# Tiles of one batch each in a sliding-window attention and feed-forward kernel

## The chip, the core and the metric

The kernel runs on one core of a Trainium2 chip. The core has TensorE (matrix products into PSUM), VectorE, ScalarE, GpSimd (POOL in the profile) and SyncE (SP), which has no arithmetic and issues DMAs; ScalarE and GpSimd issue DMAs too. Each engine works through its own instructions in order; semaphores order the engines among each other. The metric is the time on the device in microseconds (us), as a median of several runs.

## The reference

Eight batches of eight heads, 576 rows, head size 64. Each row attends to itself and the 63 rows ahead of it in its own batch; the result goes through a feed-forward block with a gate.

```python
scores = scale * np.matmul(q, k.transpose(0, 1, 3, 2))
rel = pos[:, None] - pos[None, :]
mask = (rel >= 0) & (rel < 64)
attn = softmax(where(mask, scores, -1e9))
x = matmul(attn, v).transpose(0, 2, 1, 3).reshape(4608, 512)
g = x @ w_gate                                  # 512 x 1536
out = (g / (1 + exp(-g)) * (x @ w_val)) @ w_out # 1536 x 512
```

Inputs and output are float32. The kernel computes in bfloat16 and adds up in float32.

## The kernel before, in words

The 4608 rows (8 x 576) are cut into nine tiles of 512 rows in the order of memory. As 576 is no multiple of 512, tile t holds the last 64t rows of batch t-1 and the first 512-64t rows of batch t (`segments`). So a tile's first query block needs the last 64 keys of the tile before it (`kT[(t - 1) % 2]`, line 205 ff.), and one place of the mask moves from tile to tile: GpSimd clears it and restores it in `maskp` (`clear_part`, `restore_part`).

Every tile does the same: load q, k and v; turn q and k so that the head dimension lies on partitions; per pair of heads u (0 to 3) the scores (18 matmuls of 64 keys against 64 or 128 queries, `scores`), exp on ScalarE, the mask; the sums over keys by a product with ones, and their inverse by Ln and Exp on ScalarE (`sums`); the values (16 matmuls, `values`) and the multiplication into `xT`; twelve blocks m of gate and value (`gate_value`, eight matmuls each, then Silu on ScalarE and a multiplication on VectorE into `hT`); four output blocks (`project`, twelve matmuls each). V is held twice: `v1` as it is, and `v2` shifted by 64 rows, so that a window of 128 keys is always 128 partitions; `shift_v` makes `v2` from `v1`.

The order is written by hand; each engine works in the order of the code. The first two tiles (`TURNED = 2`) are loaded as rows and turned on TensorE (`transposes`), and their mask is added in PSUM from `bias`; the later ones are loaded so that VectorE's 32x32 transposition turns them (`load_q`, `load_k`, `turn`), and their mask is a product.

The opening is lines 325 to 437. SP, and ScalarE for some of k, load q and k of tile 0 as float32; ScalarE, VectorE and GpSimd cast them. GpSimd loads tile 1's q and k with a cast on the way (`load_later`), casts v of tile 0, and then loads the weights of gate and value in four blocks of 384 columns with tile 1's v between the second and the third. The shifts of v are DMAs on SP (`shift_dma`). On TensorE eight turns (two tiles, four head pairs) alternate with scores and sums; then come tile 0's values and gate/value blocks 0 and 1. Only after tile 1's last sums does ScalarE load the table for Silu (`set_silu`) and free the PSUM buffers of the gate:

```python
    begun.append(gate_value(0, 1))
    load_qk(2)
    for c in range(2):
        weights_o(6 * c, 6 * c + 6)
    set_silu()
    for m in range(12):
        (begun[m] if m < 2 else gate_value(0, m))()
        if 7 <= m < 11:
            values(1, m - 7, ps_a.tile([P, 2, 512], FP32, name="ao_ps", tag="a")[:, 0])
```

From then on a tile's scores and values alternate with the output blocks of the tile before, and the loads for later tiles stand ahead of the gate/value blocks in GpSimd's and SP's queues. The PSUM buffers: two pairs in `ps_a` (tag a: scores, sums), two each of the tags g and v in `ps_f` (turns, gate, value, output).

Of the kernel before, what the change touches and what calls it, by code (L numbers as in the profile page):

```python
# [8 lines left out]
P = 128  # L9
# [8 lines left out]
def kernel(  # L18
# [14 lines left out]
    TURNED = 2  # L33

# [3 lines left out]
    cast = ctx.enter_context(tc.tile_pool(name="cast", bufs=4))  # L38
# [10 lines left out]
    kT = [cst.tile([P, 4, 512], BF16, name=f"kT{i}") for i in range(2)]  # L49
# [3 lines left out]
    ones = cst.tile([P, D], BF16, name="ones")  # L53
    tri = cst.tile([P, 2, 64], BF16, name="tri")
    bias = [cst.tile([P, 2, 4, 4, 2, 16], BF16, name=f"bias{i}") for i in range(2)]
    maskp = cst.tile([P, 2, 16, 4, 2, 4], BF16, name="maskp")

    def segments(t):

        n0 = 64 * t  # L60
        segs = []
        if n0 > 0:
            segs.append((0, t - 1, S - n0, min(n0, 512)))
        if n0 < 512:
            segs.append((n0, t, 0, 512 - n0))
        return segs
# [9 lines left out]
    def load_runs(eng, dst, src, t, hs, e):  # L76

        w = P * e
        for off, b, s0, n in segments(t):
            o, s, left = off, s0, n  # L80
            while left:
                m = min(left, w - o % w)
                x = o % w // e
                eng.dma_start(  # L84
                    dst[x:x + m // e, :, o // w].rearrange("r h e d -> r h (e d)"),
                    src[b, hs, s:s + m].rearrange("h (r e) d -> r h (e d)", e=e),
                )
                o, s, left = o + m, s + m, left - m

    def load_q(t):  # L90

        q_s = stage.tile([P, 4, 16 * D], BF16, name="q_s", tag="q")
        w = 16 * D - 32
        for a in range(2):
            for c in range(2):
                for off, b, s0, n in segments(t):
                    p0 = 64 * a + 32 * c + off // 16
                    nc.gpsimd.dma_start(  # L98
                        q_s[p0:p0 + n // 16, :, 0:w],
                        q[b, a:H:2, s0:s0 + n].rearrange("u (r e) d -> r u (e d)", e=16)  # L100
                        [:, :, 32 * c:32 * c + w],
                    )
        return q_s

    def load_k(t):

        k_s = stage.tile([P, 4, 4, 4 * D], BF16, name="k_s", tag="k")
        w = 4 * D - 32
        for a in range(2):
            for c in range(2):  # L110
                for off, b, s0, n in segments(t):
                    o, s, left = off, s0, n
                    while left:
                        m = min(left, P - o % P)
                        p0 = 64 * a + 32 * c + o % P // 4
                        nc.gpsimd.dma_start(  # L116
                            k_s[p0:p0 + m // 4, o // P, :, 0:w],
                            k[b, a:H:2, s:s + m].rearrange("u (r e) d -> r u (e d)", e=4)
                            [:, :, 32 * c:32 * c + w],
                        )  # L120
                        o, s, left = o + m, s + m, left - m
        return k_s

    def load_qk(t):
        staged[t] = (load_q(t), load_k(t))

    def load_v(eng, dst, t):

        for off, b, s0, n in segments(t):
            o, s, left = off, s0, n  # L130
            while left:
                m = min(left, P - o % P)
                eng.dma_start(
                    dst[o % P:o % P + m, o // P],
                    v[b, :, s:s + m].rearrange("h r d -> r h d"),
                )
                o, s, left = o + m, s + m, left - m

    def stage_v(t):
        staged[t, "v"] = stage.tile([P, 4, H, D], FP32, name="v_f", tag="v", bufs=1)  # L140
        load_v(nc.sync, staged[t, "v"], t)

    def cast_v(t, *which):
        for i in which or range(4):
            nc.gpsimd.tensor_copy(v1[t % 2][:, i], staged[t, "v"][:, i])  # L145

    def shift_v(t, copy):

        a, b, z = v1[t % 2], v2[t % 2], v1[(t - 1) % 2]
        if t:  # L150
            copy(b[64:128, 0], z[64:128, 3])
        copy(b[64:128, 1:4], a[64:128, 0:3])
        copy(b[0:64], a[0:64])
# [13 lines left out]
    def transposes(t, u):  # L167
# [4 lines left out]
        for i, (x, h0) in enumerate(staged.pop((t, u))):  # L172
            for e in range(4):
                for h in range(2):
                    nc.tensor.transpose(
                        tp[64 * h:64 * h + 64, i, P * e:P * e + P],
                        x[:, h0 + h, 0, e, :] if i == 0 else x[:, h0 + h, e // 2, e % 2, :],
                        identb[:],
                    )
        nc.vector.tensor_copy(queries[t][:, u, :], tp[:, 0, :])  # L180
        nc.vector.tensor_copy(
            kT[t % 2][:, u, :].rearrange("p (g r e) -> p g e r", g=2, e=2),
            tp[:, 1, :].rearrange("p (g e r) -> p g e r", g=2, e=2),
        )

    def turn(t, u):

        if u == 0:
# [5 lines left out]
        )  # L194
        nc.vector.transpose(  # L195
            kT[t % 2][:, u, :].rearrange("r (g x e) -> r g e x", g=4, e=4),
# [3 lines left out]
    def scores(t, u):  # L200
# [4 lines left out]
        for j in range(-1, 8):  # L205
            c = j % 2
            lo, hi = max(0, j), min(8, j + 2)
            src = kT[t % 2] if j >= 0 else kT[(t - 1) % 2]
            for h in range(2):
# [3 lines left out]
                    src[r, u, 64 * (j % 8):64 * (j % 8) + 64],  # L213
                    blocks(qT[r], t, lo, hi),
                    start=t >= TURNED or j < 1, stop=t >= TURNED,
                )
        if t < TURNED:
            for c in range(2):
                for h in range(2):
# [3 lines left out]
                        bias[t][r, c ^ h].rearrange("r e i c x -> r (e i c x)"),  # L223
# [3 lines left out]
        if t >= TURNED:  # L227
# [3 lines left out]
                maskp[:].rearrange("r h e i c x -> r (h e i c x)"),  # L231
            )
        weights[t, u] = E

    def part(ap, t):

        i, c = divmod(t, 2)
        r = slice(64 - 64 * c, P - 64 * c)
        return ap[r, :, :, i, c, :], tri[r, c, :]

    def clear_part(t):
        nc.gpsimd.memset(part(maskp, t)[0], 0.0)

    def restore_part(t):
        dst, src = part(maskp, t)
        for h in range(2):
            nc.gpsimd.tensor_copy(dst[:, h], src.rearrange("r (x e) -> r e x", e=16))  # L247

    def sums(t, us, d_ps):

        for i, u in enumerate(us):
            for h in range(2):
                nc.tensor.matmul(  # L253
                    d_ps[64 * h:64 * h + 64, i], ones[:], weights[t, u][:, h, :]
                )
# [7 lines left out]
    def values(t, u, o_ps):  # L263
# [3 lines left out]
        for m in range(8):  # L267
            for h in range(2):
                nc.tensor.matmul(  # L269
                    blocks(o_ps[64 * h:64 * h + 64], t, m, m + 1),  # L270
                    (v1 if m % 2 else v2)[t % 2][:, m // 2, 2 * u + h, :],
# [8 lines left out]
    def gate_value(t, m):  # L280
        if m == 0:
            hT[t] = hpool.tile([P, 12, 512], BF16, name="hT", tag="hT")
        g_ps = ps_f.tile([P, 512], FP32, name="g_ps", tag="g")
        v_ps = ps_f.tile([P, 512], FP32, name="v_ps", tag="v")
        for ps, w in ((g_ps, wg), (v_ps, wv)):
            for c in range(4):
                nc.tensor.matmul(  # L287
                    ps[:], w[:, c, P * m:P * m + P], xT[t][:, c, :],
# [3 lines left out]
        def finish():  # L292
            sg = fsb.tile([P, 512], FP32, name="sg", tag="sg")
            nc.scalar.activation(sg[:], g_ps[:], AF.Silu)  # L294
            nc.vector.tensor_mul(hT[t][:, m, :], sg[:], v_ps[:])  # L295
# [3 lines left out]
    def project(t, s):  # L299
# [8 lines left out]
        rows = out[512 * t:512 * t + 512]  # L308
        if t < TURNED:
            nc.sync.dma_start(rows.rearrange("(r e) f -> e r f", e=4)[s], os_[:])  # L310
        else:
            for i in range(4):
                eng = nc.scalar if t == NT - 1 and i % 2 else nc.sync
                eng.dma_start(
                    rows.rearrange("(r e) f -> e r f", e=16)[4 * s + i], os_[32 * i:32 * i + 32]
                )
# [4 lines left out]
    def set_silu():  # L321
# [4 lines left out]
        stage.tile([P, H, 1, 4, D], FP32, name="q_f", tag="q"),  # L326
        stage.tile([P, H, 2, 2, D], FP32, name="k_f", tag="k"),
    ]
    for u in range(4):
        hs = slice(2 * u, 2 * u + 2)  # L330
        load_runs(nc.sync, raw[0][:, hs], q, 0, hs, 4)
        load_runs(nc.scalar if u < 2 else nc.sync, raw[1][:, hs], k, 0, hs, 2)
    stage_v(0)
    set_exp()
    make_identity(nc, identb[:])
    nc.vector.memset(ones[:], 1.0)
    nc.vector.memset(v2[0][64:128, 0], 0.0)
    nc.vector.memset(kT[1][:, :, 448:512], 0.0)
    nc.gpsimd.memset(tri[:], 1.0)
    for a in range(2):  # L340
# [9 lines left out]
    later = [  # L350
        stage.tile([P, H, 1, 4, D], BF16, name="q_n", tag="q"),
        stage.tile([P, H, 2, 2, D], BF16, name="k_n", tag="k"),
    ]

    def load_later(i, half):
        hs = slice(4 * half, 4 * half + 4)
        load_runs(nc.gpsimd, later[i][:, hs], (q, k)[i], 1, hs, (4, 2)[i])

    load_later(0, 0)
    load_later(1, 0)  # L360
    for x in range(2):
        for c in range(2):
            nc.vector.tensor_scalar(
                bias[0][:, x, :, 0, c], tri[:, c ^ x].rearrange("r (x e) -> r e x", e=4),
                1e9, -1e9, op0=ALU.mult, op1=ALU.add,
            )
    for i in (1, 2):
        nc.vector.tensor_copy(
            bias[0][:, :, :, i:2 * i].rearrange("r s e i c x -> r (s e) (i c x)"),
            bias[0][:, :, :, 0:i].rearrange("r s e i c x -> r (s e) (i c x)"),  # L370
        )
    nc.vector.tensor_copy(bias[1][:], bias[0][:])
    for t in range(2):
        i, c = divmod(t, 2)
        for h in range(2):
# [141 lines left out]
```

## Time and profile before

| what | value |
|---|---|
| median of 5 runs | 346.88 us (344.58 to 348.87) |
| the profiled execution's own time | 346.88 us |
| its span in the profile | 345.2 us |
| TensorE matmul busy | 328.4 us, 95% of the span |
| VectorE, ScalarE, GpSimd busy | 201.4, 162.2, 140.9 us |
| read from HBM, written to it | 50.14 MB, 9.44 MB |
| gate and value matmuls (864) | 223.7 us busy |
| output matmuls (432) | 99.0 us busy |

The profile is of one execution, with times in us from the start of its span. Busy time of TensorE is modelled: matmuls are pipelined, so one of 512 columns shows about 380 ns, while a run of them starts one every 0.216 us (eight in 1.73 us). PEclk is the clock that the throttle granted, in tenths; it has no record ahead of its first change, so it reads 1.00 until 17.6 us, although the eight transpositions of one operand take 0.64 us until 17.2 us and 0.41 us from 17.95 us on. In a list of instructions the first two columns are start and duration, `x8` is how many were merged, and the bracket tells the engine's idle time before and what ended it. In a table of stages each row has the stretch, its length, the busy time of TensorE, of its weight loads, of VectorE, ScalarE and GpSimd (each with the count of instructions), the granted clock, the share of the DMA engines and GB/s. DMA bytes count at their destination: a load that casts to bfloat16 reads twice that.

### The profile page before, as it was taken

Reading aid. Unit: us, or ns where it says so; the run is one execution under the profiler, and the core shown is the slowest. Engines: PE = TensorE matmul, PEld = TensorE weight load, DVE = VectorE, ACT = ScalarE, POOL = GpSimd, SP = SyncE. Lnnn points to the kernel's source line nnn. Section 1 sums busy time; section 2 is a strip of 40 time slices with the busy share of each in tenths; the row PEclk is TensorE's granted clock in tenths of the full one; section 3 lists DMA queues with packets and bytes.
Section 4 is the critical chain, followed back from the end, with each engine's and each line's share of the span. In section 5 each row is a group of like instructions: output and inputs, shape, how many; then the busy total and the mean of one; then the engine's idle time right before and its main releaser. Section 6 shows DMA issues by size and latency. Waiting matters only on the chain.

```text
span 345.2 us, 7045 instructions
## 1 busy us (share of the span) xinstructions
PE 328.4 (95%) x2752; PEld 156.0 (45%) x2752; DVE 201.4 (58%) x300; ACT 162.2 (47%) x226; POOL 140.9 (41%) x267
## 2 busy tenths in 40 slices
PE   1887999999999999999999999999999999999994
PEld 1553444444444454445444544444444544454441
DVE  4353356675447665767576757674767566753331
ACT  2496233353343376337633763377336733673310
POOL 6695369357376218641853186408600200000000
PEclk9999899999999999999999999999999999999999
DMA  8999999999989617980799179817971230031013
GB/s 216 229 185 184 225 166 123 172 189 146 219 166 241 106 30 135 233 137 24 140 218 150 33 135 235 130 32 121 242 136 33 63 92 2 10 83 32 1 31 92
DMA packets 80450, 44.36 MB, mean 129 GB/s; under 512 B 60832, under 2 KB 74656, under 8 KB 80416
## 3 DMA queue, kind: packets, MB, share of 16 engines
q0 software_dynamic: 39376, 20.37, 46.0%
q1 hardware_dynamic: 39568, 22.49, 25.8%
q10 hardware_dynamic: 1472, 1.05, 1.2%
q8 instruction: 21, 0.34, 0.4%
q14 instruction: 13, 0.11, 0.1%
HBM read 50.14 MB, written 9.44 MB: 173 GB/s over the span
## 4 chain that ended last, share of the span: by engine, by line
PE 90%; DMA 5%; POOL 2%; ACT 1%; DVE 1%; issue 0%; ACTq 0%; SPq 0%; DVEq 0%; POOLq 0%
PE o_ps L302 28%; PE g_ps L287 27%; PE v_ps L287 27%; DMA k_f<-in_k_dram 3%; PE ao_ps L269 3%; PE d_ps L253 2%; PE s_ps L211 2%; DMA v<-v 2%; DVE xT L274 1%; POOL v L145 1%; POOL k_n L84 1%; ACT L322 0%; POOL q_n L84 0%; ACT r L259 0%; ACT r L258 0%; DVE os__4461 L307 0%
## 5 line engine op out<-in xcount | busy, mean ns | idle before, releaser
L294 ACT ACTIVATE sg<-g_ps 128x512 f32<-128x512 f32 x108 | 64.4, 597 | 119.6 <-PE g_ps L287 94.7
L295 DVE TENSOR_TENSOR hT<-sg,v_ps 128x512 bf16<-128x512 f32 x108 | 74.9, 694 | 74.6 <-PE v_ps L287 68.6
L287 PE MATMUL g_ps<-xT,wg 128*128 128x512 bf16 x432 | 112.0, 381 | 2.4 <-ACT sg L294 2.3
L287 PE MATMUL v_ps<-xT,wv 128*128 128x512 bf16 x432 | 111.7, 381 | 0.0
L302 PE MATMUL o_ps<-wo,hT 128*128 128x512 bf16 x432 | 99.0, 380 | 0.0
L116 POOL DMA_DIRECT2D k_s<-in_k_dram x124 | 65.9, 537 | 31.9 <-DMA q_s<-in_q_dram 18.8
L287 PEld LDWEIGHTS <-wg 128*128 128x128 bf16 x432 | 42.0, 98 | 53.2 <-issue 4.1
L287 PEld LDWEIGHTS <-wv 128*128 128x128 bf16 x432 | 42.5, 98 | 51.9 <-issue 1.2
L302 PEld LDWEIGHTS <-hT 128*128 128x128 bf16 x432 | 39.7, 98 | 45.1
L226 ACT ACTIVATE E<-s_ps 128x1024 bf16<-128x1024 f32 x36 | 35.3, 1020 | 16.9 <-PE s_ps L211 9.4
L274 DVE TENSOR_TENSOR xT<-ao_ps,r 128x512 bf16<-128x512 f32 x36 | 24.7, 690 | 22.2 <-ACT r L259 20.5
L195 DVE STREAM_TRANSPOSE kT<-k_s 128x512 bf16<-128x512 bf16 x28 | 35.9, 1283 | 0.0
L98 POOL DMA_DIRECT2D q_s<-in_q_dram x52 | 28.8, 561 | 15.0 <-DMA wv<-in_moe_w_val_dram 5.4
L258 ACT ACTIVATE r<-d_ps 128x512 f32<-128x512 f32 (+1 forms) x32 | 20.6, 644 | 26.5 <-PE d_ps L253 24.4
L247 POOL COPY maskp<-tri 64x64 bf16<-64x64 bf16 x12 | 3.1, 286 | 64.9 <-DVE E L228 64.8
L228 DVE TENSOR_TENSOR E<-E,maskp 128x1024 bf16<-128x1024 bf16 x28 | 19.4, 692 | 12.0 <-ACT E L226 11.5
L259 ACT ACTIVATE r<-r 128x512 f32<-128x512 f32 (+1 forms) x32 | 21.9, 683 | 1.0
L191 DVE STREAM_TRANSPOSE qT<-q_s 128x512 bf16<-128x512 bf16 x28 | 19.7, 704 | 0.0
L145 POOL CAST v<-v_f 128x512 bf16<-128x512 f32 x28 | 16.1, 611 | 6.3 <-DMA v_f<-in_v_dram 4.9
L269 PEld LDWEIGHTS <-v 128*64 128x64 bf16 x576 | 13.7, 112 | 6.1 <-issue 2.2
L269 PE MATMUL ao_ps<-E,v 128*64 128x64 bf16 x576 | 15.1, 196 | 0.7 <-DMA v<-v 0.5
L253 PE MATMUL d_ps<-E,ones 128*64 128x512 bf16 x72 | 14.0, 406 | 0.8 <-ACT E L226 0.8
(82 smaller groups left out, 137.0 us busy)
## 6 DMA issues: line engine op xcount, KB each, us to landing
v_f<-in_v_dram SPq DMA_DIRECT2D x25, 256.0 KB, 6.9
k_s<-in_k_dram POOLq DMA_DIRECT2D x100, 56.0 KB, 5.4
v<-v SPq DMA_DIRECT2D x9, 256.0 KB, 6.2
v<-v SPq DMA_DIRECT2D x9, 192.0 KB, 5.4
wg<-in_moe_w_gate_dram POOLq DMA_DIRECT2D x4, 384.0 KB, 9.1
wv<-in_moe_w_val_dram POOLq DMA_DIRECT2D x4, 384.0 KB, 11.0
wo<-in_moe_w_out_dram POOLq DMA_DIRECT2D x2, 768.0 KB, 9.1
q_s<-in_q_dram POOLq DMA_DIRECT2D x8, 186.0 KB, 6.6
```

Source lines behind the costliest of these rows:

```text
L98: nc.gpsimd.dma_start(q_s[p0:p0 + n // 16, :, 0:w], q[b, a:H:2, s0:s0 + n].rearrange("u (r e) d -> r u (e d)", e=16) [:, :, 32 * c:32 * c ...
L116: nc.gpsimd.dma_start(k_s[p0:p0 + m // 4, o // P, :, 0:w], k[b, a:H:2, s:s + m].rearrange("u (r e) d -> r u (e d)", e=4) [:, :, 32 * c:32 ...
L195: nc.vector.transpose(kT[t % 2][:, u, :].rearrange("r (g x e) -> r g e x", g=4, e=4), k_s[:, :, u].rearrange("r g (e d) -> r g e d", d=D)[ ...
L226: nc.scalar.activation(E[:], s_ps[:], AF.Exp, scale=0.125)
L253: nc.tensor.matmul(d_ps[64 * h:64 * h + 64, i], ones[:], weights[t, u][:, h, :])
L259: nc.scalar.activation(x, x, AF.Exp, scale=-1.0)
L269: nc.tensor.matmul(blocks(o_ps[64 * h:64 * h + 64], t, m, m + 1), (v1 if m % 2 else v2)[t % 2][:, m // 2, 2 * u + h, :], blocks(E[:, h, :] ...
L274: nc.vector.tensor_mul(xT[t][:, u, :], o_ps[:], inverse.pop((t, u)))
L287: nc.tensor.matmul(ps[:], w[:, c, P * m:P * m + P], xT[t][:, c, :], start=(c == 0), stop=(c == 3),)
L294: nc.scalar.activation(sg[:], g_ps[:], AF.Silu)
L295: nc.vector.tensor_mul(hT[t][:, m, :], sg[:], v_ps[:])
L302: nc.tensor.matmul(o_ps[:], hT[t][:, c, P * s:P * s + P], wo[:, c, :], start=(c == 0), stop=(c == 11),)
```

## The change

Tiles are now batches: tiles 0 to 6 hold rows 0 to 511 of batches 0 to 6, tile 8 those of batch 7, and tile 7 (`LAST`) the last 64 rows of all eight batches. No tile needs another's keys: the first score matmul is against zeros, and the mask no longer changes. The tile of tails has a mask of its own, 16 pieces of 64 keys against 64 queries per head (32 matmuls instead of 18), a second set of keys (`k_l`, loaded at tile 2, turned on VectorE in tiles 3 to 6 after block 8), and takes v from both `v1` and `v2`.

In the opening all loads of q, k (both tiles) and v (tile 0) are float32 on SP (two on ScalarE), by pairs of heads in the order of need, with halves of v between; GpSimd casts tile 1's too. The weights come in blocks of 128, 256, 384, 384 and 384 columns; the first stands in GpSimd's queue between the casts, tile 1's v between the fourth and the fifth. V of tiles 0 and 1 is shifted by VectorE copies in place of DMAs. TensorE gets matmuls on a tile of ones (`keep_warm`) whose result is not used. Scores of the last pair stand ahead of tile 0's values, the last sums after block 0, and block 2 is begun early in a `ps_a` buffer.

```diff
+    LAST = NT - 2
...
+    def batch(t):
+        return t if t < LAST else t - 1
...
-    def shift_v(t, copy):
-
-        a, b, z = v1[t % 2], v2[t % 2], v1[(t - 1) % 2]
-        if t:
-            copy(b[64:128, 0], z[64:128, 3])
-        copy(b[64:128, 1:4], a[64:128, 0:3])
-        copy(b[0:64], a[0:64])
+    def shift_v(t, copy, lo=0, hi=4):
+
+        a, b = v1[t % 2], v2[t % 2]
+        top = min(hi, 3)
+        copy(b[64:128, lo + 1:top + 1], a[64:128, lo:top])
+        copy(b[0:64, lo:hi], a[0:64, lo:hi])
...
+        if t == LAST:
+            pieces = [
+                (c, b, b + 1, kT[t % 2 if b < 4 else 2], P * (b % 4) + 64 * c)
+                for b in range(8) for c in range(2)
+            ]
+        else:
+            pieces = [(1, 0, 1, None, 0)] + [
+                (j % 2, j, min(8, j + 2), kT[t % 2], 64 * j) for j in range(8)
+            ]
...
+    def load_pair(t, u):
+        hs = slice(2 * u, 2 * u + 2)
+        for x, src in zip(raw[t], (q, k)):
+            eng = nc.scalar if t == 0 and u < 2 and src is k else nc.sync
+            load_runs(eng, x[:, hs], src, t, hs)
+
     for u in range(4):
+        load_pair(0, u)
+    load_pair(1, 0)
+    load_pair(1, 1)
+    load_v(nc.sync, staged[0, "v"], 0, (0, 1))
+    load_pair(1, 2)
+    load_v(nc.sync, staged[0, "v"], 0, (2, 3))
+    load_pair(1, 3)
...
+    def keep_warm(n):
+        for _ in range(n):
+            nc.tensor.matmul(warm[0:D], ones[:, 0:D], ones[:])
+
+    keep_warm(8)
...
     for u in range(4):
+        cast_pair(0, u)
+    cast_pair(1, 0)
+    cast_pair(1, 1)
+    cast_v(0, (0, 1))
+    cast_pair(1, 2)
+    weights_gv(0, 128)
+    cast_v(0, (2, 3))
+    cast_pair(1, 3)
+    weights_gv(128, 384)
+    weights_gv(384, 768)
+    weights_gv(768, 1152)
+    load_v(nc.gpsimd, v1[1], 1)
+    weights_gv(1152, 1536)
...
+    turn_pe(0)
+    for i in range(1, 6):
+        turn_pe(i)
+        score(i - 1)
         if i > 2 and i % 2:
+            sum_pair(i - 3)
+        if i > 3:
+            keep_warm(2)
+    shift_v(0, nc.vector.tensor_copy, 0, 2)
+    score(5)
+    keep_warm(2)
+    turn_pe(6)
+    score(6)
+    sum_pair(4)
+    keep_warm(2)
+    shift_v(0, nc.vector.tensor_copy, 2, 4)
+    turn_pe(7)
+    score(7)
+    for u in range(4):
+        values_of(0, u)
+    begun.append(gate_value(0, 0))
+    sum_pair(6)
     begun.append(gate_value(0, 1))
+    begun.append(gate_value(0, 2, ps_a.tile([P, 2, 512], FP32, name="gv_ps", tag="a")))
...
     for m in range(12):
-        (begun[m] if m < 2 else gate_value(0, m))()
+        (begun[m] if m < 3 else gate_value(0, m))()
+        if m == 6:
+            shift_v(1, nc.vector.tensor_copy)
...
-            restore_part(t)
-            if t + 1 < 8:
-                clear_part(t + 1)
...
+            if m == 8 and 3 <= t < 7:
+                turn_k(kT[2], k_l, t - 3)
```

## The prediction

> **What bounds the kernel now.** I read the page first, then the busy time by stage, then the opening instruction by instruction. The page:
>
> ```profile
> span 345.2 us, 7045 instructions
>
> DMA  8999999999989617980799179817971230031013
> PE 90%; DMA 5%; POOL 2%; ACT 1%; DVE 1%; issue 0%; ACTq 0%; SPq 0%; DVEq 0%; POOLq 0%
> ```
>
> TensorE is 90% of the chain that ended last; the other 10% must lie in a few places. The DMA engines are full in the first thirteen slices (112 us) only. PEclk has one dent, in the fifth slice. The stages, with TensorE's busy time (and count) first and the granted clock after POOL:
>
> ```profile
> 30.00:35.00 5.00, 2.73 (x14) 1.09 (x12) 1.29 (x2) 4.33 (x6) 3.30 (x6) 0.97 2.07 169
> 35.00:40.00 5.00, 5.00 (x17) 1.94 (x16) 1.38 (x2) 1.05 (x3) 1.36 (x3) 0.69 1.27 240
> 40.00:45.00 5.00, 5.00 (x25) 2.29 (x24) 2.06 (x3) 1.61 (x4) 1.15 (x2) 1.00 1.23 204
> 260.00:300.00 40.00, 40.00 (x379) 19.02 (x378) 27.42 (x38) 22.80 (x32) 2.74 (x6) 1.00 0.16 40
> ```
>
> From 40 us to 340 us TensorE never pauses (the list of its waits is empty after 36 us), so there only its own instructions count. Time can be won before 40 us. TensorE and ScalarE there:
>
> ```profile
> 21.57 0.41 PE L175 MATMUL tp<-identb,q_n 128*64 128x128 bf16 x8
> ...
> 26.76 1.30 PE L287 MATMUL g_ps<-xT,wg 128*128 128x512 bf16 x4
> ...
> 30.27 1.03 PE L287 MATMUL v_ps<-xT,wv 128*128 128x512 bf16 x4
> 33.57 1.02 PE L287 MATMUL g_ps<-xT,wg 128*128 128x512 bf16 x4 [2.27 <-ACT sg L294]
> ...
> 35.83 1.91 PE L287 MATMUL g_ps<-xT,wg 128*128 128x512 bf16 x4
> ...
> 38.70 1.03 PE L287 MATMUL g_ps<-xT,wg 128*128 128x512 bf16 x4
> ```
>
> I call the eight turns of (tile, head pair) T0 to T7, and G0 to G11 tile 0's gate/value blocks. T7 starts at 21.57, G0 at 26.76, G1 ends at 31.3; 2.27 us of idling follow, because both PSUM pairs are full until ScalarE has done this:
>
> ```profile
> 29.51 1.02 ACT L258 ACTIVATE r<-d_ps 128x1024 f32<-128x1024 f32 x1 [2.40 <-PE d_ps L253]
> 30.57 1.06 ACT L259 ACTIVATE r<-r 128x1024 f32<-128x1024 f32 x1
> 31.63 1.28 ACT L322 ACT_TABLE_LOAD   x1
> ```
>
> Then the clock is halved from about 34.7 to 38.1 us (0.50 in the windows of 1 us), so G2 and G3 take 5.13 us, not 2 x 1.73 = 3.46. At 38.70 (G4) the steady flow begins. All after it takes 345.2 - 38.7 = 306.5 us and is TensorE's own. The question is when G4 starts after the change.
>
> **The opening, part by part.** *Loads.* Before, SP and ACT carry 2.1 MB of q and k and 1 MB of v of tile 0, and POOL the 2.1 MB of tile 1, cast on the way; the last of these lands at 20.7 us. After, SP carries all 5.2 MB in the order of need. Rates from the windows of 1 us: 344 to 359 GB/s at 3 to 5 us with packets of 1 KB and 512 B (k now has 1 KB too), so 1.5 us for a pair of q and k (0.52 MB); 216 to 251 GB/s at 13 to 16 us, where v moves in 256-byte packets, so 2.2 us for half of v. First data at 1.9 us; six pairs to 10.8, half of v to 13.0, a pair to 14.5, half of v to 16.7, the last pair to 18.2, and about 0.9 us until it is told: 19.1. POOL casts half of v from 18.1 (two at 0.6), then q and k of the last pair (two at 0.6): 20.5. T7 can begin with q, so it starts at about 20.1, 1.5 us earlier than now. POOL's first small weight block (issued near 16.6) meets only the tail of this; met in full it would cost 1.5 us.
>
> *From T7 to G4.* Turn and two VectorE copies 1.75 us (21.57 to 23.31 now), scores and bias 0.65, the first values 0.5, four multiplications into xT 2.58 (25.04 to 27.62 now), then 5 of G0's 8 matmuls 1.1: G0 is issued at T7+6.55. Now G0 starts at T7+5.2; its wv block lands only at about 27.3. The last sums follow (0.45), so the logarithm starts at T7+7.2. From the logarithm to the first free PSUM pair is 4.06 us now (29.51 to 33.57) and stays so: G3 can start at T7+11.3. G1 and G2 (in ps_a) fill TensorE until T7+10.5; the pause is 0.8 us instead of 2.27, at full clock. G4 starts at T7+13.0 = 33.1 us, against 38.70. **Gain 5.6 us**: 1.5 from T7, 1.7 from the clock, 2.4 from the order and the third PSUM pair.
>
> *Weights.* They now queue on POOL behind tile 1's casts: issue at 20.5 instead of 19.04, except a first 0.5 MB. The stream's rate shows where POOL waits for a landing:
>
> ```profile
> 29.57 0.74 POOL L157 DMA_DIRECT2D wv<-in_moe_w_val_dram  x1 [1.22 <-DMA wg<-in_moe_w_gate_dram]
> 32.01 0.74 POOL L157 DMA_DIRECT2D wg<-in_moe_w_gate_dram  x1 [1.70 <-DMA wv<-in_moe_w_val_dram]
> ...
> 45.41 0.59 POOL L98 DMA_DIRECT2D q_s<-in_q_dram  x1 [2.03 <-DMA wv<-in_moe_w_val_dram]
> ```
>
> 0.79 MB took 2.0 and 2.4 us: 0.36 MB/us. So the columns up to 384 land at about 26 (G1 wants them at 27.2), up to 768 at 30.4 (G3: 31.5), up to 1152 at 34.8 (G6: 36.6), tile 1's v, 3.4 us as now, at 38.2 (wanted at 39.0), the rest at 42.6 (G9: 43.2; now it lands at 45.1). Each comes 0.6 to 1.8 us in time; lateness beyond that is lost one for one. I take nothing. The shifts of v by DMA, 0.9 MB in this stretch, are gone, which helps. Tile 2's keys, all issued at 55.3 now and turned at 59.4, move with the stream by 2 to 3 us and VectorE can lag 1.2 us: nothing, if the gain stays under 6.
>
> *V on VectorE.* For tile 1 the two copies stand after G6's multiplication: 1536 and 2048 elements, by the nearest row (bias 128x1024, 0.49 us) 1.7 us. VectorE ends that multiplication at 39.0 and the copies at 40.7; values(1,0) could start at 40.1. Cost 0.6 (between 0, if faster, and 1.7). Queued behind them: the multiplications that free PSUM. Tile 0's copies lie in waits for loads: nothing.
>
> **The rest.** *The tile of tails* has 32 score matmuls per head pair instead of 18. Now two head pairs together:
>
> ```profile
> 295.27 0.66 PE L211 MATMUL s_ps<-qT,kT 64*64 64x64 bf16 x36
> 295.86 2.76 PE L302 MATMUL o_ps<-wo,hT 128*128 128x512 bf16 x12
> ```
>
> 36 in 0.59 us, 16.4 ns each: 4 x 14 x 16.4 ns = 0.9 us. The Trainium skill (TensorE: Matmul & The Clock Gate, "Wait — 56ns, not 53.3ns?") speaks against the change: starts never follow closer than about 25 ns, however small the matmul. That would give 1.4 us; but these run in pairs on two halves of the array, so the row decides: 0.9. *Its other keys* add a 1.28 us transposition on VectorE in four tiles. Blocks 7 to 9 there then have 3 x 0.69 + 2.0 + 1.28 = 5.35 us of VectorE work in 5.19 us of TensorE's; its multiplication of block 8 still ends 0.9 us before TensorE needs the buffer. Nothing; uncovered, up to 5.1. *POOL* loses the mask edits and their waits (64.8 us, on no path), gains sixteen key loads (0.54 each), nine copies and eight v loads; it is half idle from 100 us and done by 270: nothing. SP sheds a shift per tile: nothing. A score against zeros replaces one against old keys: nothing.
>
> **Sum.** 5.6 - 0.6 - 0.9 = 4.1 us. Span 341.1; this execution took 346.88 us, 1.7 more than its span, and is the median of the five: **342.8 us**, -1.2%.
>
> **The rivals.**
> - *Half clock again (0.17).* The skill's same page (Part 1) has the clock halve after an idle window of about 3.4 us. This trace halved it after a pause of 2.27 us, with 1.1 us of matmuls run again before it fell. After, T7 waits for the last load, with some 1.5 to 2 us of little work before it beside the two warming matmuls: by the rule nothing, by the row 3.4 us at half clock, 1.7 us lost: 344.5. For it: the first full clock in this trace comes at 17.6 us, after 12 us of small matmuls (eight transposes 0.64 us, then 0.41). Against: the warming matmuls.
> - *Loads at the old average (0.14).* 5.2 MB by 20.7 us is 0.28 MB/us, not 0.3 to 0.36; then the last pair lands at 20.7, T7 starts near 22 and the weights move with it: 1.9 us lost, 344.7.
> - *Better (0.08).* Copies under cover, T7 a us earlier: 341.2.
> - *Slower (0.06): VectorE waits for tile 1's v.* The copies sit in VectorE's queue ahead of all multiplications; now v lands at 35.1 behind half of the weights, and only values wait for it. After it stands behind three quarters. If it lands where those stand now in the old stream, 41.0 to 45.1 us, VectorE and soon TensorE stand still for 2 to 6 us. From 43.1 on the gain is gone; at 45.1 it is 348.9; with the clock halved in such a pause 350.6.
> - The forecast (0.55) has 341.6 to 344.2.
>
> The range reaches over the clock and load cases, and leaves out the late v: 340.9 to 345.6. One per cent (3.5 us) is about what a measurement can tell from no change; 343.4 lies just above the forecast, so faster 0.64, same 0.31, slower 0.05.
>
> **What would show it.** Right: T7 near 20 us, G4 near 33, a pause of about 0.8 us ahead of G3, full clock from G0 on, no TensorE wait later but some tenths at values(1,0), 0.9 us more in the scores before the last tile but one. Wrong: G1, G3 or G6 waiting for wg or wv, VectorE's copy waiting for v, a clock below 1 between 20 and 40 us, TensorE waiting around block 9 of tiles 3 to 6.

## The result, and the profile after

The changed kernel takes 344.25 us (median of 24 runs, 343.04 to 346.69), the kernel before 346.68 us (45 runs, 344.58 to 349.63). The ratio is 0.9938, with an interval of 0.992 to 0.9957: 2.4 us less, inside the predicted range and short of the 1% that the prediction took as its bound: 0.6% where 1.2% was forecast. The interval does not reach 1, so the gain is clear of the noise. The profiled execution of after took 344.38 us, with a span of 342.3 us: 2.9 us less span than before, where 4.1 were forecast, and 2.1 us around the span in place of 1.7.

The page of after, in the lines that answer to those of before:

```profile
span 342.3 us, 7129 instructions
...
PEclk9989999999999999999999999999999999999998
DMA  7999999998799939919970799889501230020013
...
PE 87%; DMA 5%; DVE 2%; POOL 1%; ACT 1%; SPq 1%; issue 1%; DVEq 0%
```

The dent in PEclk has moved from the fifth slice to the third. TensorE has a smaller share of the chain than before (87% for 90%) although the span is shorter: there are waits that were not there. The stages of after, with the columns of the table of before:

```profile
25.00:30.00 5.00, 5.00 (x46) 2.25 (x41) 1.47 (x3) 1.30 (x2) 3.57 (x5) 0.84 1.24 166
30.00:35.00 5.00, 4.46 (x22) 1.95 (x20) 2.16 (x4) 4.24 (x6) 2.05 (x3) 1.00 1.48 194
35.00:40.00 5.00, 5.00 (x25) 2.25 (x23) 1.88 (x4) 1.79 (x3) 2.68 (x5) 1.00 1.90 179
40.00:45.00 5.00, 4.57 (x51) 2.09 (x49) 3.73 (x7) 1.19 (x2) 1.61 (x4) 1.00 1.19 209
```

Between 30 and 40 us TensorE now loses 0.54 us, where before it lost 2.27, and the clock is full there. But 0.43 us are lost after 40 us, where before nothing was. TensorE from T7 to G4:

```profile
20.18 0.97 PE L175 MATMUL tp<-identb,qk_b 128*64 128x128 bf16 x16
21.98 0.22 PE L219 MATMUL s_ps<-qT,zero 64*64 64x64 bf16 x2 [0.83 <-DVE qT L179]
22.58 0.41 PE L219 MATMUL s_ps<-qT,kT 64*64 64x128 bf16 x16 [0.38 <-DVE kT L180]
...
25.80 1.41 PE L286 MATMUL g_ps<-xT,wg 128*128 128x512 bf16 x4
...
28.00 0.62 PE L248 MATMUL d_ps<-E,ones 128*64 128x512 bf16 x4
...
30.30 1.03 PE L286 MATMUL gv_ps<-xT,wg 128*128 128x512 bf16 x4
...
32.73 1.02 PE L286 MATMUL g_ps<-xT,wg 128*128 128x512 bf16 x4 [0.54 <-ACT sg L293]
...
34.45 1.03 PE L286 MATMUL g_ps<-xT,wg 128*128 128x512 bf16 x4
```

T7 starts at 20.18 us (20.1 was forecast), G2 runs in the third buffer (`gv_ps`), the pause ahead of G3 is 0.54 us. G4 starts at 34.45: 4.25 us earlier than before, not 5.6. ScalarE shows where the rest is:

```profile
28.67 1.02 ACT L253 ACTIVATE r<-d_ps 128x1024 f32<-128x1024 f32 x1 [3.83 <-PE d_ps L248]
29.72 1.06 ACT L254 ACTIVATE r<-r 128x1024 f32<-128x1024 f32 x1
30.79 1.28 ACT L324 ACT_TABLE_LOAD   x1
```

The logarithm starts at T7+8.49, not T7+7.2. From there to G3 it is 4.06 us, to the hundredth the interval that the prediction took from before. So nearly all that is missing at G4 lies between T7 and the logarithm. Two causes are seen. First the clock, in windows of 1 us (the number after POOL's count):

```profile
23.00:24.00 1.00, 1.00 (x36) 0.86 (x33) 0.11 (x1) 0.18 (x1) 1.00 (x2) 0.59 1.39 186
24.00:25.00 1.00, 0.57 (x23) 0.48 (x21) 1.00 (x2) 0.84 (x1) 1.00 (x2) 0.50 1.46 196
25.00:26.00 1.00, 1.00 (x28) 0.77 (x23) 0.80 (x3) 0.00 (x0) 1.00 (x3) 0.50 1.35 133
26.00:27.00 1.00, 1.00 (x4) 0.35 (x3) 0.68 (x2) 0.00 (x0) 1.00 (x2) 0.71 1.08 134
```

It is halved from 23.2 to 26.6 us, 3.4 us as before, only in another place. Second, GpSimd and VectorE ahead of T7's scores; here is VectorE:

```profile
19.06 1.77 DVE L152 COPY v<-v 64x512 bf16<-64x512 bf16 x1 [0.69 <-POOL v L146]
20.87 0.73 DVE L153 COPY v<-v 64x1024 bf16<-64x1024 bf16 x1
21.53 0.40 DVE L179 COPY qT<-tp 128x512 bf16<-128x512 bf16 x1
```

GpSimd casts the last pair's k until 20.68, so the turn ends at 21.15; and VectorE is then still copying v, so T7's q begins to leave PSUM at 21.53 only.

TensorE's waits for others in after, in all, times and longest; before, the list was empty after 36 us:

```profile
PE g_ps L286 <- DVE os__1921 L306: 0.9, 1, 0.9
...
PE g_ps L286 <- ACT sg L293: 0.5, 1, 0.5
...
PE ao_ps L264 <- DVE v L153: 0.4, 1, 0.4
```

The second is the pause ahead of G3, the third is values(1,0). The first ends at 134.3 us, one block after tile 2's last output block: `g_ps` needs the PSUM buffer that VectorE's copy `os__1921` has to empty. Nothing in the prediction speaks of it.

### The profile page after: what moved, and what is told of

The parts are those of the page before. It is cut to its first block, busy times and chain, and to the rows that moved or that the text cites. A ratio compares the mean times of both kernels' runs of the same rounds, so it can differ in the third digit from the quotient of the medians.

```text
span 342.3 us, 7129 instructions
## 1 busy us (share of the span) xinstructions
PE 330.2 (96%) x2824; PEld 156.5 (46%) x2824; DVE 209.7 (61%) x309; ACT 162.3 (47%) x226; POOL 142.3 (42%) x253
## 4 chain that ended last, share of the span: by engine, by line
PE 87%; DMA 5%; DVE 2%; POOL 1%; ACT 1%; SPq 1%; issue 1%; DVEq 0%
PE o_ps L301 27%; PE g_ps L286 27%; PE v_ps L286 26%; PE ao_ps L264 3%; PE s_ps L219 3%; PE d_ps L248 2%; DMA v_f<-in_v_dram 2%; DMA out_dram<-os__1786 2%; DMA k_f<-in_k_dram 2%; SPq L318 1%; DVE v L152 1%; POOL qk_b L393 0%; DVE v L153 0%; SPq L73 0%; ACT L324 0%
## 5 line engine op out<-in xcount | busy, mean ns | idle before, releaser
L294 DVE TENSOR_TENSOR hT<-sg,v_ps 128x512 bf16<-128x512 f32 x107 | 74.1, 693 | 65.3 <-PE v_ps L286 59.1
L286 PE MATMUL g_ps<-xT,wg 128*128 128x512 bf16 x428 | 110.3, 380 | 1.5 <-DVE os__1921 L306 0.9
L286 PE MATMUL v_ps<-xT,wv 128*128 128x512 bf16 x428 | 109.8, 379 | 0.0
L107 POOL DMA_DIRECT2D k_s<-in_k_dram x112 | 60.5, 549 | 32.1 <-DMA q_s<-in_q_dram 21.6
L146 POOL CAST v<-v_f 128x512 bf16<-128x512 f32 x24 | 15.0, 633 | 29.6 <-DMA v_f<-in_v_dram 27.9
L236 DVE TENSOR_TENSOR E<-E,mask 128x1024 bf16<-128x1024 bf16 x24 | 16.8, 698 | 10.7 <-ACT E L234 10.7
L87 POOL DMA_DIRECT2D q_s<-in_q_dram x24 | 13.1, 552 | 22.5 <-DVE qT L190 13.2
L264 PE MATMUL ao_ps<-E,v 128*64 128x64 bf16 x576 | 15.8, 200 | 0.9 <-DVE xT L270 0.4
L219 PE MATMUL s_ps<-qT,kT 64*64 64x128 bf16 (+1 forms) x640 | 12.9, 211 | 0.8 <-DVE kT L180 0.8
```

Of the source, the lines that this page charges most:

```text
L107: nc.gpsimd.dma_start(k_s[p0:p0 + 32, g, :, 0:w], k[b, a:H:2, s:s + P].rearrange("u (r e) d -> r u (e d)", e=4) [:, :, 32 * c:32 * c + w],)
L219: nc.tensor.matmul(blocks(s_ps[64 * c:64 * c + 64, h], t, lo, hi), zero[r] if src is None else src[r, u, x:x + 64], blocks(qT[r], t, lo, h ...
L264: nc.tensor.matmul(blocks(o_ps[64 * h:64 * h + 64], t, m, m + 1), (v1, v2)[m // 4][t % 2][:, m % 4, 2 * u + h, :] if t == LAST else (v2, v ...
L286: nc.tensor.matmul(ps, w[:, c, P * m:P * m + P], xT[t][:, c, :], start=(c == 0), stop=(c == 3),)
L294: nc.vector.tensor_mul(hT[t][:, m, :], sg[:], v_ps)
```

## Experiments

Each expectation is what was put down before the run. All ratios are against the kernel before, with runs on the same chip; its median was 346.6 to 347.0 us in these.

### The new tiles with the old opening

The tiles of the change, with the opening of before: its loads, casts and order, its DMAs for v, two blocks begun. Against the changed kernel, the last lines of the edit (the loads, casts and order are left out here):

```diff
     begun.append(gate_value(0, 1))
-    begun.append(gate_value(0, 2, ps_a.tile([P, 2, 512], FP32, name="gv_ps", tag="a")))
...
-        (begun[m] if m < 3 else gate_value(0, m))()
-        if m == 6:
-            shift_v(1, nc.vector.tensor_copy)
+        (begun[m] if m < 2 else gate_value(0, m))()
```

> The new tiles with the opening of before (loads, casts, weights, shifts by DMA, two blocks begun, no warming matmuls). Theory: the whole gain is the opening's; the tiles of their own cost the pause of 0.9 us at the end of tile 2 (16 loads of the extra keys in the way of an output block) and 0.1 us in the scores of the tails, so 347.7 us, 0.3% above before, with the 0.9 us wait of TensorE for an output copy near 135 us. Rival: the steady part profits from the tiling (no mask edits, fewer shifts) and gives part of the gain: 345.5 us or less.

Measured: 346.63 us (22 runs), before 346.99; ratio 1.0 [0.9976, 1.0024]. The tiles alone are worth nothing, within 0.8 us. TensorE's wait behind tile 2's outputs, expected at 0.9 us, is 0.4 us there. The new scores can be read in the change's own profile, where the tile of tails has its scores between gate/value blocks and an output block:

```profile
257.80 0.71 PE L219 MATMUL s_ps<-qT,kT 64*64 64x64 bf16 x64
258.44 2.76 PE L301 MATMUL o_ps<-wo,hT 128*128 128x512 bf16 x12
```

64 matmuls in 0.64 us, 10 ns each, where 36 took 0.59 us before. Twice the matmuls, but half the queries in most: per head 1024 columns of queries pass in both forms (16 x 64; or 64 + 7 x 128 + 64). What the tails' scores cost is 0.05 us for two head pairs, 0.1 in all, not 0.9.

### More warming

```diff
     turn_pe(6)
+    keep_warm(2)
     score(6)
...
     turn_pe(7)
+    keep_warm(4)
     score(7)
```

> The changed kernel with two more warming matmuls after turn T6 and four after T7, where TensorE waits for VectorE's copies. Theory: the half clock of 3.4 us, from 23.2 us on, comes from the thin work between T6 and the last scores; with it filled the clock stays full, values and G0 run 1.3 us faster and the median falls to 343.2 us (ratio to the changed kernel 0.997). Rival: the clock isn't on the path, since G0 waits for the multiplications on VectorE anyway: no change, 344.2 us.

Measured: 343.91 us (6 runs), ratio 0.993 [0.9907, 0.9952]. The mean granted clock is 0.9965 or more in all six executions, against 11 of the change's 25 whose clock is recorded, so this did keep the clock up. The time hardly moved. In its profile, G4:

```profile
34.21 1.03 PE L286 MATMUL g_ps<-xT,wg 128*128 128x512 bf16 x4
```

0.24 us earlier than in after, at full clock. T7 started at 20.55 there, k's half at 21.30 (it waited for GpSimd's cast), the logarithm at 28.42: T7+7.87 at full clock. So 0.67 us are missing against the forecast there too, and the clock has no part in them.

### No warming at all

```diff
-    keep_warm(8)
...
-        if i > 3:
-            keep_warm(2)
...
     score(5)
-    keep_warm(2)
...
     sum_pair(4)
-    keep_warm(2)
```

> The changed kernel with none of the warming matmuls. Theory: T7 stays at 20.2 us, since loads and casts set it; before, the clock came to full at 17.6 us without any warming, so at most another window of 3.4 us at half clock falls on values and the first blocks: 344.3 to 346 us. Rival: the warming carries the gain: 346.5 us or more.

Measured: 343.86 us (14 runs), ratio 0.9935 [0.9914, 0.9956]. The clock is below 0.9965 in 11 of 14 executions, in none of the six with more warming: so the warming does act on the clock. But the median is that of the change. My expectation that it costs time to leave them out was wrong. At full clock (0.9965 or more) the three executions without warming took 342.90 us in the mean, the change's eleven 343.76; that is a hint, from few executions, that the warming also costs some of what it brings.

### The tails' other keys a tile later

The other keys are loaded at tile 3 in place of tile 2, and two of them are turned in tile 6.

```diff
-        if t == 2:
+        if t == 3:
             k_l = load_k(
...
-            if m == 8 and 3 <= t < 7:
-                turn_k(kT[2], k_l, t - 3)
+            if (t, m) in ((4, 8), (5, 8), (6, 5), (6, 8)):
+                turn_k(kT[2], k_l, 2 if (t, m) == (6, 5) else 3 if t == 6 else t - 4)
```

> The changed kernel with the extra keys of the tails loaded one tile later (tile 3) and turned in tiles 4, 5 and twice in 6. Theory: the 0.9 us pause of TensorE after tile 2's output blocks is the output DMA delayed by those 16 loads beside the loads for tile 4; it goes, DMA is at 0.8 of full in tile 3, and the median falls to 343.4 us. Rival 1: the pause only moves one tile on: 344.2 us. Rival 2: the pause is of the loads for tile 4 (v above all) and stays where it is: 344.2 us.

Measured: 342.75 us (6 runs), ratio 0.9911 [0.9882, 0.994]; span 341.1 us. The wait of 0.9 us is gone from TensorE's list. What it was is seen in GpSimd's and SyncE's queues and on VectorE. After:

```profile
111.53 8.02 POOL L107 DMA_DIRECT2D k_l<-in_k_dram  x15 [0.83 <-DMA k_s<-in_k_dram]
...
126.15 2.14 POOL L87 DMA_DIRECT2D q_s<-in_q_dram  x4
```

```profile
124.93 3.11 SPq L318 DMA_DIRECT2D out_dram<-os__1786  x4
```

```profile
133.57 0.69 DVE L306 COPY os__1921<-o_ps 128x512 f32<-128x512 f32 x1 [2.14 <-DMA out_dram<-os__1786]
```

And with the keys loaded later:

```profile
117.41 2.15 POOL L87 DMA_DIRECT2D q_s<-in_q_dram  x4 [4.87 <-DVE qT L190]
```

```profile
124.75 1.74 SPq L318 DMA_DIRECT2D out_dram<-os__1760  x4
```

In after GpSimd issues the other keys for 8 us, copies the second mask and casts v. Tile 4's q, which stands behind, is issued at 126.15, 1.2 us after the start of an output of tile 2 whose four issues take 3.11 us. This output lands so late that the fourth output copy, which needs the same buffer, waits 2.14 us, and TensorE behind it 0.9. With the keys later q goes out at 117.41, 7.3 us ahead of that output, whose issues then take 1.74 us, and nothing waits, although the DMA engines are busy for more than half of 124 to 128 us, mostly with loads. So it was not the keys' own bytes but their place in the queue.

The long issue is not q's doing: in after it begins before q is issued, and the kernel before has one of 2.89 us at the same place:

```profile
128.68 2.89 SPq L314 DMA_DIRECT2D out_dram<-os__1768  x4
...
130.89 4.43 POOL L98 DMA_DIRECT2D q_s<-in_q_dram  x8
```

There q follows 2.2 us behind the output's start, and no copy waits. So a long issue alone does not make the wait; q close behind it does. Whether q close behind a promptly issued output would, no run shows. Over all the profiles it holds: the seven with the new tiles and the keys at tile 2 have TensorE waiting there for 0.3 to 1.2 us, the three with the keys later and the two with the old tiles not at all.

The intervals of this run and of the change overlap, so the 1.5 us between their medians are not certain as a time; that the wait is gone is.

### Two blocks begun, not three

```diff
-    begun.append(gate_value(0, 2, ps_a.tile([P, 2, 512], FP32, name="gv_ps", tag="a")))
...
-        (begun[m] if m < 3 else gate_value(0, m))()
+        (begun[m] if m < 2 else gate_value(0, m))()
```

> The changed kernel with two gate/value blocks begun ahead of the table load instead of three. Theory: TensorE then waits from the end of G1 (30.3 us in the profile after) to the first free PSUM pair (32.7 us), 2.4 us instead of 0.5, so G2 starts where G3 starts now: 1.7 us lost, and in some executions the clock is halved after it as in the kernel before: 345.9 to 347.5 us. Rival: the weights are what G3 waits for, so the third block only moves the wait: 344.3 us.

Measured: 346.81 us (21 runs), before 346.62; ratio 1.0004 [0.9983, 1.0024]. With everything else of the change in place nothing is left of the gain. TensorE ahead of what is now G2:

```profile
32.72 1.20 PE L286 MATMUL g_ps<-xT,wg 128*128 128x512 bf16 x4 [2.27 <-ACT sg L293]
...
35.42 1.74 PE L286 MATMUL g_ps<-xT,wg 128*128 128x512 bf16 x4
```

The old pause of 2.27 us is back, 0.85 us earlier than before, and the clock is halved behind it again (33.4 to 36.9 us).

### Before, with only the third block

```diff
     begun.append(gate_value(0, 1))
+    begun.append(gate_value(0, 2, ps_a.tile([P, 2, 512], FP32, name="gv_ps", tag="a")))
...
-        (begun[m] if m < 2 else gate_value(0, m))()
+        (begun[m] if m < 3 else gate_value(0, m))()
```

> The kernel before, with one edit: gate/value block 2 is begun ahead of the table load in a ps_a buffer. Theory from the run with two blocks: this buffer alone carries the gain; TensorE's pause of 2.3 us ahead of G2 shrinks to about 0.5 us ahead of G3, and with it goes the half clock that follows the long pause: 1.7 us, or up to 3.4 us where the clock had fallen: 344.2 us, as much as the whole change. Rival: it needs the new order of loads and casts to have its weights in time, or tile 0's later start eats it: 346 us or more.

Measured: 344.88 us (22 runs), before 346.74; ratio 0.9952 [0.9931, 0.9974]. One added block gives 1.9 of the change's 2.4 us in the median, with the old tiles, loads and casts, and v shifted by DMA. TensorE's G3, G4 and the second half of G6:

```profile
33.25 1.02 PE L290 MATMUL g_ps<-xT,wg 128*128 128x512 bf16 x4 [0.54 <-ACT sg L297]
...
34.97 1.03 PE L290 MATMUL g_ps<-xT,wg 128*128 128x512 bf16 x4
...
40.06 1.04 PE L290 MATMUL v_ps<-xT,wv 128*128 128x512 bf16 x4 [0.61 <-DMA wv<-in_moe_w_val_dram]
```

The same pause of 0.54 us as in after, and G4 only 0.52 us later (0.7 later than in the runs with more warming and with the keys later, whose opening was at full clock like this one). But it isn't kept: the old weight stream is too late for G6 (0.61 us), TensorE waits for VectorE at 59.9 us (0.46), and from G4 to the end it is 307.9 us, not 306.5. So the expectation's rival, that the weights need the new order, was right for a part.

The executions sorted by their mean granted clock say the same. At 0.9965 or more the third block alone takes 344.80 us in the mean (14 executions), the kernel before in the same session 345.11 (10): 0.3 us. Below that it takes 345.4 (8) and the kernel before 347.5 (17). So alone it brings 2 us where the clock falls, and hardly anything at full clock.

### The last sums ahead of block 0

```diff
-    begun.append(gate_value(0, 0))
     sum_pair(6)
+    begun.append(gate_value(0, 0))
     begun.append(gate_value(0, 1))
```

> The changed kernel with tile 1's last sums ahead of G0 instead of behind it. Theory: the chain logarithm, exponential, table load, Silu starts 1.8 us earlier, the pause of 0.54 us ahead of G3 goes: 343.7 us, ratio to the changed kernel 0.9985. Rival: the sums now wait for the last exp, TensorE loses there what it wins: 344.2 us. A third way: G3 comes so early that it waits for its weights (landed at 31.9 us): 344.0 us.

Measured: 344.46 us (8 runs), ratio 0.9934 [0.9909, 0.996]. The pause ahead of G3 is gone and G4 starts 1.5 us earlier than in after, yet the time is the same. TensorE's G4, and VectorE at tile 2's keys:

```profile
32.96 1.03 PE L286 MATMUL g_ps<-xT,wg 128*128 128x512 bf16 x4
```

```profile
56.45 1.32 DVE L197 STREAM_TRANSPOSE kT<-k_s 128x512 bf16<-128x512 bf16 x1 [2.23 <-DMA k_s<-in_k_dram]
```

VectorE now stands 2.23 us for tile 2's keys, with a multiplication queued behind that frees PSUM, and TensorE waits 1.2 us for it. The wait behind tile 2's outputs is 1.2 us, 0.3 more than in after. So what is won at G4 is lost to the loads, most of it some 25 us later. I had expected it to be kept.

### The last pair's casts off GpSimd

```diff
-    cast_pair(1, 3)
     weights_gv(128, 384)
...
     score(6)
+    nc.scalar.copy(staged[1][:, 0, 6:8], raw[1][0][:, 6:8])
+    nc.vector.tensor_copy(staged[1][:, 1, 6:8], raw[1][1][:, 6:8])
     sum_pair(4)
```

> The changed kernel with the casts of tile 1's last pair on ScalarE (q) and VectorE (k), behind the scores of T6, instead of on GpSimd behind a weight issue and two casts of v. Theory: T7's two halves are set by GpSimd's row of work (k cast ends at 20.7 to 21.3 us), and the second weight block can be issued 1.1 us earlier; T7 to G0 move 0.6 us forward: 343.6 us. Rival: the last pair lands only at about 20 us, so nothing moves: 344.2 us, with ScalarE's and VectorE's casts waiting for the load.

Measured: 344.6 us (9 runs), ratio 0.9935 [0.9901, 0.997]. T7 starts at 20.82: VectorE waits 1.54 us for the last k to land, until 20.04, and ScalarE has q cast only at 20.77. The load itself lands so late that taking GpSimd's casts away leaves T7 waiting for it. Alone this moves nothing.

### The parts together

Four edits at once: keys later, sums first, the second copy of v after block 5 in place of 6, and the added warming.

```diff
-        if m == 6:
+        if m == 5:
             shift_v(1, nc.vector.tensor_copy)
```

> The changed kernel with the extra keys loaded a tile later, the sums ahead of G0, tile 1's shift of v one block earlier (behind G5's multiplication) and the more evenly spread warming matmuls. Theory: 0.9 us (pause after tile 2) + 0.5 (ahead of G3) + 0.4 (values(1,0) waiting for the shift) off the 344.2 us of the changed kernel: 342.4 us, and no wait of TensorE over 0.3 us after G0. Rival: VectorE, at the shift, waits for tile 1's v (landed at 39.2 us, wanted at 38.3 us or earlier), and the gates pay for it: 343 us or more.

Measured: 343.42 us (5 runs), ratio 0.9893 [0.9857, 0.993]. VectorE still waits 1.8 us for tile 2's keys, and TensorE waits 0.5 us for wv and 0.8 for VectorE, where no wait over 0.3 was expected. The next kernel leaves the added warming out and takes the casts off GpSimd, which then issues the weights 1.2 us earlier (19.41 in place of 20.62 us), and tile 2's keys behind them:

> The combined version (extra keys a tile later, sums ahead of G0, tile 1's shift of v one block earlier), here without the added warming matmuls and with the last pair's casts on ScalarE and VectorE, so that GpSimd issues the large weight blocks about 1 us earlier. Theory: in the combined version TensorE waits 0.5 us for wv and 0.8 us for VectorE, whose turn of tile 2's keys waits 1.8 us for their load; the earlier stream takes most of these 1.3 us: 342.2 us against 343.4. Rival: GpSimd's 0.54 us for each of the sixteen key loads sets it, not the stream: 343.4 us.

Measured: 341.88 us (6 runs, 340.88 to 343.39), before 346.74; ratio 0.9868 [0.9835, 0.9901]. TensorE and VectorE there:

```profile
31.67 1.03 PE L286 MATMUL g_ps<-xT,wg 128*128 128x512 bf16 x4
...
33.40 1.03 PE L286 MATMUL g_ps<-xT,wg 128*128 128x512 bf16 x4
```

```profile
54.08 1.28 DVE L197 STREAM_TRANSPOSE kT<-k_s 128x512 bf16<-128x512 bf16 x1
```

No pause ahead of G3, no wait for the keys, and no TensorE wait for another engine after G0. From G4 to the end it is 339.7 - 33.40 = 306.3 us, the 306.5 of before. Its interval and that of the change do not overlap: it beats both kernels. The sums alone ran into tile 2's keys and tile 2's outputs; the casts alone left the pause ahead of G3 where it was. Together with the tails' keys out of the way and the earlier copy of v they bring 2.4 us beside the change's 2.4. Of that, the keys alone had brought 1.5 (342.75 us); no run takes the other edits out one by one, so their shares are read from the waits that are gone.

## Why the prediction was half right

The sum, term by term, from the two profiled executions:

| term | predicted, us | measured, us |
|---|---|---|
| T7 earlier | 1.5 | 1.4 |
| half clock gone (in after it comes back elsewhere) | 1.7 | about 1.0 |
| order and third PSUM pair | 2.4 | about 1.85 |
| G4 earlier | 5.6 | 4.25 |
| v copies at values(1,0) | -0.6 | -0.43 |
| tails' scores | -0.9 | -0.1 |
| tails' other keys on GpSimd's queue | 0 | -0.9 |
| span | 4.1 | 2.9 |
| around the span | 0 | -0.4 |
| time | 4.1 | 2.5 |

**T7 to the logarithm is the first step that failed.** It was put at 7.2 us and measured 8.49. By rows: the turn and its two copies took 2.40 us, not 1.75 (0.3 for k's cast, 0.3 for VectorE's copy of v, which the prediction had laid "in waits for loads: nothing"); the first values, the multiplications into xT and G0 took 0.7 us more than put down, and they lie in the half-clock stretch. The split of 1.0 and 1.85 in the table is this 0.7. In the runs with more warming and with the keys later, whose opening was at full clock, T7 to the logarithm was 7.87 and 7.74 us. So of the 1.29 us missing there, 0.6 to 0.75 go with the half clock, and 0.5 to 0.7 are a term that was put too low. T7 itself came later in these two runs (20.55 and 20.75), so their G4 stands at 34.2 and 34.3 all the same; in the nine profiles with the new opening T7 is at 20.2 to 20.8, and one execution does not fix it closer.

**The clock.** The prediction took the half-clock stretch of before as a fixed cost of 1.7 us and gave its return a chance of 0.17. It is in fact there in some executions of either kernel and not in others. Mean times by mean granted clock (a stretch of 3.4 us at half clock takes 0.005 off the mean; the executions of before are those of the first experiments):

| mean granted clock | before, us (executions) | after, us (executions) |
|---|---|---|
| 0.9965 or more | 345.34 (12) | 343.76 (11) |
| 0.9935 to 0.9965 | 347.29 (15) | 344.38 (9) |
| lower | 347.42 (8) | 345.89 (5) |

At full clock the change is worth 1.6 us, where the forecast without its clock term is 2.4. It is worth more where the clock falls: before, that costs 2 us, behind the pause, where TensorE is the bound; after, the first step down costs 0.6. The rival "half clock again" names a time, 344.5, near the result, and its stretch is in the profile; but in the median it is about a third of the reason: at full clock the change took 343.76, 0.5 us less than its median, and the forecast was missed by 1.45. The rivals on loads and on tile 1's v were false: T7 was at 20.18, and VectorE's second copy waited for no load.

**"POOL gains sixteen key loads ... nothing" is the second step that failed.** The prediction asked whether GpSimd had time for them, and it has. It did not ask what is queued behind them. Tile 4's q came to lie close behind an output of tile 2, and TensorE lost 0.9 us in this execution; with the keys later the wait is gone. The mask edits and their waits, which the change drops, had a part in it: before, they held q 2.2 us behind that output; without them and without the keys in the way q goes out 7.3 us ahead of it; with the keys it comes 1.2 us behind.

**Over-priced, and so hidden in the sum:** the tails' scores (0.9 put down, 0.1 measured) and the copies at values(1,0), 0.56 + 0.69 = 1.25 us for the two, not 1.7. Together with the tails' 0.8 that is 1.0 us, which makes up for most of the 0.9 and the 0.4 that no term foresaw. So it is in part luck that the time lies within the range: the range had been widened for cases of clock and loads, of which only the clock's came, and 344.25 is just outside the forecast's own band. The copies:

```profile
40.62 0.56 DVE L152 COPY v<-v 64x1536 bf16<-64x1536 bf16 x1
41.21 0.69 DVE L153 COPY v<-v 64x2048 bf16<-64x2048 bf16 x1
```

**Right:** what bounds the kernel, the third PSUM pair as the core of the gain (two blocks: nothing left; the third block alone: 1.9 us, though almost all of it where the clock falls), the pause ahead of G3 (0.8 forecast, 0.54), the interval from the logarithm to G3, weights and tile 1's v in time. The condition on tile 2's keys, "nothing, if the gain stays under 6", was right in kind: with G4 5.74 us earlier than before, in the run with the sums first, VectorE waited 2.23 us for the keys already, and TensorE 1.2; the bound lies lower than it was put. What tiles, load order, casts, VectorE's copies of v and warming bring beside the third block cannot be told from nothing by the medians, whose intervals overlap. At full clock it can: 343.76 us (11 executions) for 344.80 (14), in different sessions whose kernels before differ by 0.2. Neither half does it alone: the opening without the third block brings nothing, and the third block without the opening 0.3 us at full clock.

**Open:** why the time around the span is 2.0 to 2.1 us in the change and four of its variants, 1.8 to 1.9 in the two with the keys later, and 1.7 before, with the old opening and with the casts off GpSimd. No row of the profile covers it.

## What to carry to other kernels

When an engine idles because all its output buffers wait for one late step elsewhere, look first for a buffer that is free at that moment: one more block of work begun gave 1.9 us here in the median. Then look whether the loads behind keep up: with the old load order most of that came only where the clock had fallen, and at full clock TensorE lost it again to weights that came 0.6 us late and to VectorE. An addition to a half idle queue costs nothing for itself, but ask what is behind it and onto whose transfers that will now fall. Once a start is moved earlier by a microsecond or two, the next load stream is the bound, so such edits are to be judged together: here two that brought nothing alone were part of doubling the gain from 2.4 to 4.9 us. Where the clock differs between executions, sort them by it before comparing.

## What the runs showed of the hardware

- **Small matmuls on quarter tiles.** 64 matmuls of 64 x 64 on 64 columns in 0.64 us, 10 ns apart in the mean. The rule that the prediction weighed (the Trainium skill, TensorE: Matmul & The Clock Gate, "Wait — 56ns, not 53.3ns?") gives 25 ns or more from start to start; the measurement decides. The prediction's own 16.4 ns from before was a price per matmul too, and wrong in the same way: 64 and 36 matmuls with the same 4096 columns took 0.64 and 0.59 us.
- **The clock gate.** In all the profiles the granted clock changes only at multiples of 3.413 us from its first change on record: the half-clock stretches last 3.41 us each, the full-clock ones between two changes 6.83, 17.07, 307.2 and 314.0 us (2, 5, 90 and 92 times 3.413). Whether a stretch comes differs from execution to execution of the same kernel: 23 of 35 before, 14 of 25 after, 0 of 6 with more warming, 11 of 14 without any. The changed kernel and the run with the keys later have the same opening; the clock fell in the profile whose changes lie at 6.10 + n x 3.41 us and not in the one with 5.15. The same page (Part 1) has a window of about 3.4 us that runs free of the kernel, which agrees with these times. But its one whole idle window isn't needed: in the window before the fall in the kernel before (31.3 to 34.7 us) TensorE paused for 2.27 us and worked the rest.
- **A copy on VectorE beside casts on GpSimd.** The copy of 64x512 bf16 took 1.77 us in after and ended 0.15 us after GpSimd's last cast; 1.22 us with the keys later; 0.67 us with the sums first, where GpSimd paused between its casts, and as long without warming, where it did not; 0.49 and 0.57 with no casts on GpSimd; and 0.29 with more warming, where GpSimd's two casts took 1.43 us instead of 1.18. The Trainium skill (SBUF — State Buffer, "SBUF: two separate sides") has a pair of ports that GpSimd shares with VectorE operations in a mode that uses both of VectorE's ports; one engine holds it for a whole instruction while the other is blocked. Most of these rows agree with that. That it was the port was not tried by a run of its own.
